# The last six pairs of output tiles of an attention and spectral-mix kernel, dealt out anew among VectorE, ScalarE, GpSimd and the queues

## Chip, cores and metric

One core of one Trainium2 chip. The metric is the device time of one execution in microseconds (us); the kernel before has a median of 435.59 us in three runs (435.58 to 436.14).

## What is computed

Sliding-window causal attention over 8 batches, 8 heads, 576 positions and 64 channels, then a spectral mix of its result. Cut to what matters here:

```python
x = attention(q, k, v)                    # window of 64, as [8, 576, 512]
X = rfft(x, axis=1)[:, :64]               # 64 modes
Y = X @ (w_r + 1j * w_i)                  # one 512 x 512 matrix per mode
y = irfft(Y, n=576, axis=1)
u = x + y
out = u + maximum(u @ w_ch, 0)
```

## The kernel before

The attention, the forward transform and the 64 modes' matmuls fill the first 397 us; they stream the weights from HBM. What this case is about is the rest: the inverse transform and the last line of the reference, which give 36 output tiles of 128 rows by 512 columns in fp32, 256 KB each.

By the time the last modes are done, the product of x with w_ch (`XW[i]`) lies ready in SBUF for every tile. A tile then needs two sums in PSUM. `pu[i]` gets the inverse transform of Y, and `ps[i]` gets XW (`tail_xw`, L812, through an identity matrix) plus the inverse transform of Y @ w_ch. With u = x + pu, the output is u + max(ps, 0).

The tiles go in 18 pairs, in the order of the list `seq`. I call the pairs 0 to 17, and the tiles of pair n "n.0" and "n.1".

- Pairs 0 to 3, 5, 7, 9 and 11 are **early** pairs (`early`, L946): most of their u stands ready in `UE[i]`, in memory that x or the transformed inputs no longer need. VectorE (DVE) adds the last modes' share (`take_u`, L857). Then, but for two tiles that DVE finishes itself (L863), ScalarE (ACT) takes max(ps, 0) out of PSUM into the output buffer (L865) and GpSimd (POOL) adds u to it there (L866).
- Pairs 4, 6, 8 and 10, between them, and 14 to 17, at the end, are **full** pairs. `full_u` (L925) makes u, `full_z` (L935) the output. In pairs 4 to 10 and in the joint pairs, TensorE (PE) adds x through an identity matrix (L876) and ACT copies u out of PSUM (L899). In pairs 14 to 17 this holds for the second tile only; for the first one DVE adds x while it copies (L897). The output, max(ps, 0) + u, is one DVE instruction for each tile (L942).
- Pairs 12 and 13 are the **joint** pairs: each of their four tiles holds the last 64 rows of two batches (tiles 8, 17, 26 and 35, whose x lies in `x4`). Their inverse transform takes two matmuls of 64 rows each (L885).
- Pair 17 is done by `last` (L955). DVE writes 17.0 whole (L968) and 17.1 in two halves.

The order of work is written out by hand, and each engine keeps to the order of its program. The output buffers are seven pairs of tiles, used in turn; the PSUM banks of pu and ps are used anew two pairs later. The outputs leave by DMAs whose issuing engine waits for the tile. SP issues them in the order of a list `plan` that is sorted by a guessed clock: 1.1 us for each early pair and 1.8 us for each other one, and 1.26 us on a second clock for each tile that POOL ends. The second tiles of pairs 12 to 16 (`by_act`) are left out of SP's list; ACT issues them in `send_behind`, one pair later, after its copies of that pair. The second half of 17.1 is ACT's too.

Of the kernel before, what the change touches and what calls it, by code (L numbers as in the profile page):

```python
# [13 lines left out]
ALU = mybir.AluOpType  # L14
ACT_F = mybir.ActivationFunctionType
# [11 lines left out]
def kernel(  # L27
# [10 lines left out]
    nc = tc.nc  # L38
    B, H, S, D = q.shape
    NM = moe_w_r.shape[0]  # L40
    DM = moe_w_ch.shape[0]
# [61 lines left out]
    for at, (grp, hb) in enumerate(steps):  # L103
        for ri in range(2):
            p = 4 * grp
# [89 lines left out]
    with tc.manual_schedule():  # L195
# [184 lines left out]
        for nm in ("k", "q", "v"):  # L380
# [9 lines left out]
                                in1=at.unsqueeze(2).to_broadcast([128, NTC, NM]), op0=ALU.mult, op1=ALU.mult)  # L390
# [7 lines left out]
                         op0=ALU.max, op1=ALU.min)  # L398
# [323 lines left out]
        UE = {}  # L722
# [52 lines left out]
        def tile_of(b, c):  # L775
            return 9 * (b // 2) + 4 * (b % 2) + c
# [25 lines left out]
        for n, pair in enumerate(seq):  # L802
            early = pair[0] in UE_OF
            clock[0] += 1.1 if early else 1.8
            for j, i in enumerate(pair):
                if early and (n, j) not in BY_DVE:
                    clock[1] = max(clock[1], clock[0]) + 1.26
                plan.append((clock[1] if early and (n, j) not in BY_DVE else clock[0], n, i))
        plan = [i for _, _, i in sorted(plan)]
        done = {}  # L810

        def tail_xw(n, js=(0, 1)):  # L812
            for i in [seq[n][j] for j in js]:
                ps[i] = bank("zt"[n % 2 == 0])
                nc.tensor.matmul(out=ps[i], lhsT=ident_r, rhs=XW[i], start=True, stop=True)  # L815

        def banks_u(n):
            for j, i in enumerate(seq[n]):
                pu[i] = bank("m" if n % 2 == 0 else "yp"[j])
# [12 lines left out]
                nc.tensor.matmul(out=ps[i], lhsT=trigLr[r, b % 2, at:at + 128], rhs=ZL[r], start=False, stop=True,  # L832
                                 skip_group_check=True, tile_position=(group_z(b), 0))

        by_act = {p[1] for p in X4 + BB[:-1]}
        behind = []

        def send(i, ut):
            done[i] = ut
            if i in by_act:  # L840
                behind.append(i)
# [9 lines left out]
        def send_behind():  # L851
            while behind:
                put_out(nc.scalar, behind.pop(0), 0, DM)

        def take_u(n):
            for i in seq[n]:
                nc.vector.tensor_tensor(out=UE[i], in0=pu[i], in1=UE[i], op=ALU.add)  # L857

        def take_z(n):
            ut = new_ut()  # L860
            for j, i in enumerate(seq[n]):
                if (n, j) in BY_DVE:
                    nc.vector.scalar_tensor_tensor(out=ut[:, j], in0=ps[i], scalar=0.0, in1=UE[i], op0=ALU.max, op1=ALU.add)  # L863
                else:
                    nc.scalar.activation(out=ut[:, j], in_=ps[i], func=ACT_F.Relu)  # L865
                    nc.gpsimd.tensor_tensor(out=ut[:, j], in0=UE[i], in1=ut[:, j], op=ALU.add)  # L866
            for j, i in enumerate(seq[n]):
                send(i, ut[:, j])

        add_x = {p[0]: "dve" for p in BB}  # L870

        def rows_u(of):
            for i in of:
                if i not in add_x:
                    for h in range(2):
                        nc.tensor.matmul(out=pu[i][:, HALF * h:HALF * h + HALF], lhsT=ident_bf, rhs=tiles[i][0][:, h],  # L876
                                         start=(h == 0), stop=True, skip_group_check=True)
                if len(tiles[i][1]) == 1:
                    (at, b), = tiles[i][1]
                    nc.tensor.matmul(out=pu[i], lhsT=trigI[:, at:at + 128], rhs=yrows(b), start=(i in add_x), stop=True,  # L880
                                     skip_group_check=True)
            for i in of:
                if len(tiles[i][1]) == 2:
                    for h, (at, b) in enumerate(tiles[i][1]):
                        nc.tensor.matmul(out=pu[i][64 * h:64 * h + 64], lhsT=trigI[:, at + 64 * h:at + 64 * h + 64], rhs=yrows(b),  # L885
                                         start=(i in add_x), stop=True, skip_group_check=True, tile_position=(0, 64 * h))
            for i in of:
                b = tiles[i][1][0][1]
                if len(tiles[i][1]) == 2 and b < NLB:
                    r = slice(group_y(b), group_y(b) + 32)  # L890
                    nc.tensor.matmul(out=pu[i], lhsT=trigX[r], rhs=YL[r], start=False, stop=True, skip_group_check=True,
                                     tile_position=(group_y(b), 0))

        def take_rows(i, ut):
            by, halves = add_x.get(i), [t.rearrange("p (h e) -> p h e", h=2) for t in (ut, pu[i])]
            if by == "dve":
                nc.vector.tensor_tensor(out=halves[0], in0=halves[1], in1=tiles[i][0], op=ALU.add)  # L897
            else:
                nc.scalar.copy(out=ut, in_=pu[i])  # L899
# [15 lines left out]
        def new_ut():  # L915
            nonlocal taken_uts
            if not homes:
                homes.append(utpool.tile([128, 2, DM], FP32, name="utx"))
            elif taken_uts == len(homes) < NUT:
                t = ringA.tile([128, 4, DM], FP32, name="ut", tag="wt")  # L920
                homes.extend([t[:, 0:2], t[:, 2:4]])
            taken_uts += 1
            return homes[(taken_uts - 1) % NUT]

        def full_u(n):  # L925
            banks_u(n)
            ut = uts[n] = new_ut()
            for of in [seq[n]] if len(tiles[seq[n][0]][1]) == 2 else [(i,) for i in seq[n]]:
                rows_u(of)
                for i in of:  # L930
                    take_rows(i, ut[:, seq[n].index(i)])
            send_behind()
            tail_xw(n)

        def full_z(n):  # L935
            ut = uts[n]
            for i in seq[n] if len(tiles[seq[n][0]][1]) == 2 else ():
                rows_z(i)
            for j, i in enumerate(seq[n]):
                if len(tiles[i][1]) == 1:  # L940
                    rows_z(i)
                nc.vector.scalar_tensor_tensor(out=ut[:, j], in0=ps[i], scalar=0.0, in1=ut[:, j],  # L942
                                               op0=ALU.max, op1=ALU.add)
                send(i, ut[:, j])

        def early(n, ahead=False):  # L946
# [8 lines left out]
        def last(n):  # L955
            banks_u(n)
            ut = new_ut()
            ut = [ut[:, j] for j in range(2)]
            for j, i in enumerate(seq[n]):
                rows_u((i,))  # L960
                take_rows(i, ut[j])
            send_behind()
            for j, i in enumerate(seq[n]):
                tail_xw(n, (j,))
                rows_z(i)
                for lo in range(0, DM, HALF * (2 - j)):
                    hi = lo + HALF * (2 - j)
                    nc.vector.scalar_tensor_tensor(out=ut[j][:, lo:hi], in0=ps[i][:, lo:hi], scalar=0.0,  # L968
                                                   in1=ut[j][:, lo:hi], op0=ALU.max, op1=ALU.add)
                    done[i] = ut[j]  # L970
                    put_out(nc.scalar if lo else nc.sync, i, lo, hi)
# [85 lines left out]
        for g in (2, 3):  # L1057
            nc.sync.dma_start(out=Zall.bitcast(FP32)[rows, 2 * g:2 * g + 2],
                              in_=ZL.bitcast(FP32)[32 * g:32 * g + 32])
        take_u(0)  # L1060
        take_z(0)
        early(1, ahead=True)
        for n in range(2, len(seq) - 1):
            if seq[n][0] in UE:
# [5 lines left out]
        assert not behind  # L1070
        assert set(plan) == set(seq[-1])

    close(*reversed(opened))
# [30 lines left out]
```

## Time and profile before

| | |
|---|---|
| median of 3 runs | 435.59 us |
| the profiled execution | 437.54 us, its span 435.4 us |
| last matmuls issued by | about 428.2 us |
| last DVE instruction ends | 431.5 us |
| last DMA issue ends (ACT, second half of 17.1) | 432.0 us |
| busy in the whole span | PE 78%, DVE 54%, ACT 41%, POOL 22% |
| POOL's last add ends | 420.9 us |

Every time below is from the start of the span. The profile takes in the first to the last instruction of the program, and the execution has some 2 us around that. DVE's 54% is an average over stages of which this one, the last 8% of the span, has its own bounds. "q" behind an engine's name (SPq, ACTq) is its sequencer: there an issue of a DMA shows, together with its wait.

### The profile page before, as it was taken

How to read it: one execution, taken by the hardware profiler on the slowest of the kernel's cores; microseconds unless marked ns; L12 is line 12 of the kernel's file. 1: busy time of each engine (PE TensorE's matmuls, PEld its weight loads, DVE VectorE, ACT ScalarE, POOL GpSimd, SP SyncE). 2: the span in 40 equal slices, each digit the busy share in tenths (PEclk: the TensorE clock that was granted, in tenths of full speed). 3: DMA queues.
4: the chain of work that ended last, by engine and by line, in shares of the span. 5: the costliest groups of instructions: out<-in, count | busy, mean ns of one | idle time of the engine just before them, and what ended most of it. 6: DMA issues, size and time to landing. Idle time of an engine off the chain costs nothing. (4 is left out here: it accounts for less than half of the span.)

```text
span 435.4 us, 11056 instructions
## 1 busy us (share of the span) xinstructions
PE 337.5 (78%) x4816; PEld 216.8 (50%) x4816; DVE 236.5 (54%) x492; ACT 180.5 (41%) x324; POOL 97.1 (22%) x146
## 2 busy tenths in 40 slices
PE   6989989999999999975217445667557769889993
PEld 3666767676767676652114222344334435445552
DVE  7588777777677676866004111312131326865776
ACT  6556757575666567531202100232121213433651
POOL 8223222222122141113102100021111211111860
PEclk8699999999999999986558655896897989999898
DMA  8999999999999999999999999999999999992796
GB/s 205 211 212 212 211 212 211 212 212 212 211 212 211 212 212 211 212 212 212 211 259 212 212 211 212 212 203 211 213 211 211 213 211 212 212 205 50 288 339 242
DMA packets 46864, 93.24 MB, mean 214 GB/s; under 512 B 2528, under 2 KB 2848, under 8 KB 46816
## 3 DMA queue, kind: packets, MB, share of 16 engines
q0 software_dynamic: 41008, 81.73, 99.2%
q1 hardware_dynamic: 4944, 9.37, 6.0%
q10 hardware_dynamic: 864, 1.44, 0.9%
q8 instruction: 37, 0.61, 0.5%
q14 instruction: 11, 0.09, 0.1%
HBM read 163.58 MB, written 9.44 MB: 397 GB/s over the span
## 5 line engine op out<-in xcount | busy, mean ns | idle before, releaser
L784 DVE CAST xw<-psz 128x512 fp32r<-128x512 f32 x36 | 24.9, 692 | 87.6 <-PE psz L618 87.6
L618 PE MATMUL psz<-wch,tr 128*128 128x512 f32 x176 | 62.2, 485 | 11.6 <-DMA wch<-in_moe_w_ch_dram 11.0
L282 DVE TENSOR_REDUCE mx<-s 128x4 fp32r<-128x512 f32 x72 | 49.5, 688 | 26.8 <-PE s L278 26.6
L586 ACT CAST tr<-ptx 128x512 fp32r<-128x512 bf16 x36 | 21.2, 589 | 98.2 <-PE ptx L611 98.2
L186 PEld LDWEIGHTS <-XQ 128*32 128x32 bf16 x448 | 18.7, 176 | 71.0 <-issue 52.5
L163 POOL DMA_DIRECT2D wi<-in_moe_w_i_dram x32 | 23.4, 732 | 104.0 <-PE psm L186 75.3
L186 PE MATMUL psm<-wi,XQ 128*32 128x512 bf16 x208 | 21.6, 486 | 31.9 <-DMA wi<-in_moe_w_i_dram 31.9
L618 PEld LDWEIGHTS psz<-wch,tr 128*128 128x128 f32 x176 | 36.3, 229 | 19.1 <-issue 11.4
L292 ACT ACTIVATE p<-s 128x512 bf16<-128x512 f32 x72 | 39.7, 603 | 13.9 <-PE s L290 13.9
L163 POOL DMA_DIRECT2D wr<-in_moe_w_r_dram x27 | 20.1, 746 | 91.7 <-PE psm L186 38.1
L186 PE MATMUL psm<-wr,XQ 128*32 128x512 bf16 x184 | 18.9, 485 | 24.2 <-DMA wr<-in_moe_w_r_dram 23.5
L235 ACT COPY kT<-tr 128x576 bf16<-128x576 bf16 x32 | 23.2, 725 | 21.8 <-PE tr L231 21.8
L278 PE MATMUL s<-kT,qT 64*64 64x128 bf16 (+1 forms) x576 | 29.5, 223 | 0.0
L270 PE MATMUL s<-mask_t,ident_bf 128*128 128x512 bf16 x72 | 28.9, 402 | 0.6
L235 ACT COPY qT<-tr 128x576 bf16<-128x576 bf16 x32 | 23.3, 728 | 11.3 <-PE tr L231 11.3
L301 DVE COPY pts<-pt 128x1024 bf16<-128x1024 bf16 (+1 forms) x40 | 25.2, 630 | 4.3 <-PE pt L298 2.6
L278 PEld LDWEIGHTS <-qT 64*64 64x64 bf16 x576 | 18.3, 108 | 18.0 <-issue 17.6
L290 PE MATMUL s<-mx,ident_r 128*128 128x512 f32 x72 | 26.8, 445 | 0.0
L235 ACT COPY vT<-tr 128x576 bf16<-128x576 bf16 x32 | 23.3, 728 | 4.3 <-PE tr L231 4.1
L218 POOL DMA_DIRECT2D rawk<-in_k_dram x15 | 8.1, 539 | 75.2 <-PE tr L231 68.8
L298 PE MATMUL pt<-ident_bf,p 128*128 128x128 bf16 x288 | 23.3, 220 | 1.8 <-issue 1.6
L643 DVE TENSOR_TENSOR stg<-psm,Yfour 128x512 bf16<-128x512 f32 x10 | 6.9, 691 | 31.1 <-PE psm L186 31.0
(242 smaller groups left out, 622.4 us busy)
## 6 DMA issues: line engine op xcount, KB each, us to landing
wi<-in_moe_w_i_dram POOLq DMA_DIRECT2D x29, 1024.0 KB, 17.9
wr<-in_moe_w_r_dram POOLq DMA_DIRECT2D x27, 1024.0 KB, 16.2
out_dram<-ut SPq DMA_DIRECT2D x25, 256.0 KB, 2.2
rawv<-in_v_dram POOLq DMA_DIRECT2D x16, 288.0 KB, 14.7
rawk<-in_k_dram POOLq DMA_DIRECT2D x15, 288.0 KB, 12.5
rawq<-in_q_dram POOLq DMA_DIRECT2D x15, 288.0 KB, 12.4
x_sb<-in_moe_w_r_dram POOLq DMA_DIRECT2D x2, 1024.0 KB, 15.8
out_dram<-utx SPq DMA_DIRECT2D x5, 256.0 KB, 2.5
```

Source lines behind the costliest of these rows:

```text
L163: nc.gpsimd.dma_start(out=w[:, to:to + len(ps)], in_=src[ps[0]:ps[-1] + 1, HALF * hb:HALF * hb + HALF, :].rearrange("g (p j) e -> p g j e" ...
L186: nc.tensor.matmul(out=ps[32 * g:32 * g + 32, 0:e], lhsT=of.rearrange("k s b m -> k (s b) m")[:, (3 * j + 1 - ri) * B:(3 * j + 5 - ri) * B ...
L235: nc.scalar.copy(out=to, in_=pt.rearrange("p j n -> p n j"))
L270: nc.tensor.matmul(out=s, lhsT=ident_bf, rhs=mask_t[:, mk], start=True, stop=True)
L278: nc.tensor.matmul(out=s[ro, t, lo:128], lhsT=lq, rhs=kT[ro, 64 * n - 64 + lo:64 * n + 64], start=False, stop=True, skip_group_check=True)
L282: nc.vector.tensor_reduce(out=mx, in_=s, axis=AX.X, op=ALU.max, negate=True)
L290: nc.tensor.matmul(out=s, lhsT=ident_r, rhs=mx.unsqueeze(2).to_broadcast([128, 4, 128]), start=False, stop=True, skip_group_check=True)
L292: nc.scalar.activation(out=p[:, 4 * c2:4 * c2 + 4, :], in_=s, func=ACT_F.Exp, scale=EX_SCALE)
L298: nc.tensor.transpose(out=pt[:, t, :], in_=st[u]["p"][:, t, :], identity=ident_bf)
L301: nc.vector.tensor_copy(out=ps[:, 0:nt, :], in_=pt[:, 0:nt, :])
L618: nc.tensor.matmul(out=pz, lhsT=tr[:, c, :], rhs=wch[:, c, :], start=(c == 0), stop=(c == NDCH - 1))
L784: nc.vector.tensor_copy(out=XW[i], in_=multiply(tr))
```

## The change

It touches the last six pairs, 12 to 17, and the order in which SP issues.

- Second tiles of pairs 12 to 16 (now `by_pool`) are finished as in the early pairs: ACT takes max(ps, 0) into the output buffer and POOL adds u there (`take_one`). Their u goes into the `UE` place of the early tiles 0.0, 0.1, 1.0, 1.1 and 2.0, which are no longer needed.
- All four joint tiles get x from DVE (`add_x`), so that PE's eight matmuls with the identity (L876) and ACT's four copies (L899) go for them.
- SP issues all whole outputs; ACT keeps only the last half. `send_behind` and `by_act` go.
- In the clock of SP's list each non-early pair counts 1.7 instead of 1.8 us, and the five second tiles go by POOL's clock. From this come SP's new places: 4.0 and 4.1 now stand ahead of 2.1, 12.0 stands ahead of 11.0 and 11.1, and from there the order is 12.0, 11.0, 11.1, 13.0, 12.1, 14.0, 13.1, 15.0, 14.1, 15.1, 16.0, 16.1, 17.0, first half of 17.1.

The core of the diff:

```diff
+        by_pool = [p[1] for p in X4 + BB[:-1]]
...
-            clock[0] += 1.1 if early else 1.8
+            clock[0] += 1.1 if early else 1.7
             for j, i in enumerate(pair):
-                if early and (n, j) not in BY_DVE:
+                pooled = (n, j) not in BY_DVE if early else i in by_pool
+                if pooled:
                     clock[1] = max(clock[1], clock[0]) + 1.26
-                plan.append((clock[1] if early and (n, j) not in BY_DVE else clock[0], n, i))
+                plan.append((clock[1] if pooled else clock[0], n, i))
...
-        by_act = {p[1] for p in X4 + BB[:-1]}
-        behind = []
...
             while plan and plan[0] in done:
-                i = plan.pop(0)
-                if i not in by_act:
-                    put_out(nc.sync, i, 0, DM)
+                put_out(nc.sync, plan.pop(0), 0, DM)
...
+        def take_one(i, ut, u, pooled):
+            if pooled:
+                nc.scalar.activation(out=ut, in_=ps[i], func=ACT_F.Relu)
+                nc.gpsimd.tensor_tensor(out=ut, in0=UE[i], in1=ut, op=ALU.add)
+            else:
+                nc.vector.scalar_tensor_tensor(out=ut, in0=ps[i], scalar=0.0, in1=u, op0=ALU.max, op1=ALU.add)
...
-        add_x = {p[0]: "dve" for p in BB}
+        add_x = {i for p in X4 for i in p} | {p[0] for p in BB}
...
         def take_rows(i, ut):
-            by, halves = add_x.get(i), [t.rearrange("p (h e) -> p h e", h=2) for t in (ut, pu[i])]
-            if by == "dve":
+            if i in by_pool:
+                ut = UE[i] = UE[seq[by_pool.index(i) // 2][by_pool.index(i) % 2]]
+            halves = [t.rearrange("p (h e) -> p h e", h=2) for t in (ut, pu[i])]
+            if i in add_x:
                 nc.vector.tensor_tensor(out=halves[0], in0=halves[1], in1=tiles[i][0], op=ALU.add)
             else:
                 nc.scalar.copy(out=ut, in_=pu[i])
...
-            send_behind()
             tail_xw(n)
...
-                nc.vector.scalar_tensor_tensor(out=ut[:, j], in0=ps[i], scalar=0.0, in1=ut[:, j],
-                                               op0=ALU.max, op1=ALU.add)
+                take_one(i, ut[:, j], ut[:, j], i in by_pool)
```

Line numbers in the text are those of the kernel before.

More of the change, by code (lines that the diff above doesn't have):

```diff
@@ L833, in late_z @@
                                  skip_group_check=True, tile_position=(group_z(b), 0))
-        by_act = {p[1] for p in X4 + BB[:-1]}
-        behind = []
         def send(i, ut):
             done[i] = ut
-            if i in by_act:
-                behind.append(i)
             while plan and plan[0] in done:
-                i = plan.pop(0)
-                if i not in by_act:
-                    put_out(nc.sync, i, 0, DM)
+                put_out(nc.sync, plan.pop(0), 0, DM)
         def put_out(by, i, lo, hi):
@@ L849, in put_out @@
             by.dma_start(out=places[S * b + at:S * b + at + 128, lo:hi], in_=done[i][:, lo:hi])
-        def send_behind():
-            while behind:
-                put_out(nc.scalar, behind.pop(0), 0, DM)
         def take_u(n):
@@ L861, in take_z @@
             for j, i in enumerate(seq[n]):
[L862 to L866, printed above, removed]
+                take_one(i, ut[:, j], UE[i], (n, j) not in BY_DVE)
             for j, i in enumerate(seq[n]):
                 send(i, ut[:, j])
-        add_x = {p[0]: "dve" for p in BB}
+        add_x = {i for p in X4 for i in p} | {p[0] for p in BB}
         def rows_u(of):
@@ L961, in last @@
                 take_rows(i, ut[j])
-            send_behind()
             for j, i in enumerate(seq[n]):
@@ L1063 @@
         for n in range(2, len(seq) - 1):
-            if seq[n][0] in UE:
+            if seq[n][0] in UE_OF:
                 early(n)
@@ L1069 @@
         last(len(seq) - 1)
-        assert not behind
         assert set(plan) == set(seq[-1])
```

## The prediction, as it was made before the changed kernel ran

> **What bounds the end now.** I read the chain of waits first, in order of time. Its columns are start, us, engine, tile and line.
>
> ```profile
> 426.52 0.24 PE pst L908
> 426.76 0.06 issue
> 426.82 0.68 DVE ut L942
> 427.50 0.61 DVE ut L897
> ...
> 431.22 0.33 DVE ut L968
> ```
>
> Up to 426.8 the chain is PE without a gap, from there DVE alone. PE's last matmul starts at 428.2; DVE ends 3 us behind it. The timeline of DVE shows how a pair is spent (start, busy us, line, tile, count, idle before):
>
> ```profile
> 422.19 1.29 DVE L942 SCALAR_TENSOR_TENSOR ut<-psz,ut 128x512 f32<-128x512 f32 x2 [0.90 <-PE psz L905]
> 423.40 0.68 DVE L897 TENSOR_TENSOR utx<-psm,x_sb 128x512 f32<-128x512 f32 x1
> 424.19 1.32 DVE L942 SCALAR_TENSOR_TENSOR utx<-pst,utx 128x512 f32<-128x512 f32 x2
> 425.43 0.68 DVE L897 TENSOR_TENSOR ut<-psy,x_sb 128x512 f32<-128x512 f32 x1
> ...
> 430.19 1.35 DVE L968 SCALAR_TENSOR_TENSOR ut<-psz,ut 128x512 f32<-128x512 f32 x3
> ```
>
> From 422.2 on DVE never rests. Starts give its prices: 0.60 from one instruction to the next (422.19, 422.80, 423.40 in the trace), 0.79 where an instruction reads what the one before it wrote (423.40 to 424.19). A plain pair costs it 0.60 + 0.79 + 0.61 = 2.0, while PE needs 1.6 (pair 14's matmuls start at 422.0, 15's at 423.6, 16's at 425.2).
>
> Next, the windows: length, then busy us (and count) of PE, PEld, DVE, ACT and POOL, granted clock, DMA share, GB/s.
>
> ```profile
> 411.00:420.00 9.00, 9.00 (x54) 5.02 (x53) 7.20 (x12) 6.33 (x13) 8.15 (x8) 1.00 1.01 373
> 420.00:423.00 3.00, 3.00 (x18) 1.54 (x17) 2.10 (x4) 1.07 (x2) 0.91 (x1) 1.00 0.95 351
> 423.00:426.00 3.00, 3.00 (x17) 1.98 (x16) 2.90 (x5) 1.09 (x2) 0.00 (x0) 1.00 0.73 269
> 426.00:429.00 3.00, 2.58 (x13) 1.52 (x11) 2.79 (x6) 1.18 (x2) 0.00 (x0) 1.00 0.89 329
> ```
>
> Two things: POOL is idle from 421 on, and ACT two thirds. And the DMA engines are full (share 1.01, 373 GB/s) until 420; they get air only because DVE then delivers too slowly. In the trace's packets, tiles that queue behind each other start 0.69 us apart (418.27, 418.96, 419.64, 420.33, 421.02).
>
> Last, the output DMAs' own view, and POOL's adds:
>
> ```profile
> DMA to landing us min/median/max: 2.0/2.1/4.5
> 418.40 2.51 POOL L866 TENSOR_TENSOR ut<-XQ,ut 128x512 f32<-128x512 f32 x2 [0.29 <-DVE XQ L857]
> ```
>
> A DMA lands 2.05 us after its issue starts if nothing is ahead of it. The last is ACT's, at 431.62, landing at 433.68; the last 1.75 us to 435.43 are final waits and stay. So the sum asks for the new last landing. A POOL add takes 1.28, one starting 1.23 after the other.
>
> **Part by part.**
>
> *PE.* Eight matmuls (L876) for the joint tiles go. In the chain they take 0.54 for pair 12 and 0.33 + 0.22 for pair 13, together 1.1. PE's start of pair 12 stays at 417.3, since what comes before is untouched. So z is complete for pairs 12 to 16 at 419.4, 421.05, 422.75, 424.35 and 425.95, and for 17.0 and 17.1 at 427.15 and 427.6. The banks it needs are free by then in the schedule below, so PE waits for nobody new.
>
> *DVE.* Five L942 go (second tiles of 12 to 16), four x adds come (joint tiles): one instruction fewer, and the waits for PE and ACT (1.16 and 0.90) close, since the adds fill them. The joint adds have no row of their own; the nearest is L897, same shapes and types, 0.68. From its last L857 (418.17) DVE is back to back: 12.0 and 12.1 add x at 418.77 and 419.37, 12.0 output 419.98; pair 13 the same at 420.6, 421.2, 421.8; then for each plain pair an add and an output, 0.60 + 0.79: outputs of 14.0, 15.0, 16.0 start at 423.2, 424.6, 426.0, 17.0 at 427.4, the halves at 428.0 and 428.3. It ends at 428.7 instead of 431.55: 2.8 earlier. Every z above is there in time, so DVE, not PE, sets this chain.
>
> *ACT and POOL.* Four copies and five issues go from ACT; five of max(ps, 0) come (L865, 0.60). They follow z: ends at 420.05, 421.75, 423.45, 425.05. There is a new wait: 16.1's u goes to a place inside x_sb, and in the built program ACT's copy waits for DVE's x add of 16.0 (ends 425.86), and DVE's x add of 17.0 waits for that copy (ends 426.5). DVE has 16.0's output to do in between, so its cost to DVE is nothing to 0.05; without that cover it would be 0.7. Queued behind ACT's wait is max(ps, 0) of 16.1, which moves to 426.4–427.0. POOL comes free at 420.9 and adds: 12.1 ready 422.1, 13.1 423.35, 14.1 424.85, 15.1 426.45, 16.1 428.4.
>
> *SP.* It takes five issues more, 0.33 each, at least 0.42 apart. It is blocked by a tile not ready: 12.0 (ready 420.66) now stands ahead of 11.0 (419.69), so SP idles from 419.0 to 420.7. 16.1 (428.4) stands ahead of 17.0 (428.05) and the first half of 17.1 (428.4): these issue at 428.42, 428.85 and 429.27. Against ACT's half, issued at 428.7, this costs half a microsecond. The earlier reordering holds 2.1 behind 4.0 and 4.1 (409.24), which leaves one tile more in the DMA queue, 0.69, until pairs 12 and 13 slow the supply. No output buffer is asked for again before some 2 us after that, so it costs nothing by itself.
>
> *DMA engines.* From 12.0 on, 13 whole tiles and two halves have to pass, 14 x 0.69 = 9.66. The first packets of 12.0 go 1.15 after its issue, at 421.85; the queue ahead is empty at about 421.5, so 0.4 is lost there. By the ready times above a gap opens only before 16.1 (0.2). So the transfers end at 421.85 + 9.66 + 0.2 = 431.7, the last landing shows at about 431.85. That is 1.8 before 433.68, not 2.8: the DMA engines, full again, give back 1.0 of DVE's gain.
>
> Sum against the profiled execution: span 435.43 - 1.83 = 433.6, execution 437.54 - 1.83 = 435.7; the median of the runs lies 1.95 below the profiled execution, so 435.59 - 1.83 = 433.8.
>
> On the transfer rate the Trainium skill has another price: DMA: Bandwidth & Descriptors, Specifications, puts the HBM limit of one core at some 358 GB/s. By that a tile takes an estimated 0.73, the 14 tiles 0.6 more, and the median would be 434.4. The windows show 373 GB/s over 9 us, and I stay with them.
>
> **Bounds of the unknown costs.** DVE's joint add: 0.60 (L897) to 0.79 (the dependent step) each; four of them, up to 0.8 late, of which the DMA queue hides part. It gives no gain below 0.60, as no DVE row of this shape is shorter. The PE saving: 0.9 to 1.1, since 0.1 of a switch of weights may pass to L885; DVE's chain hides it. POOL beside DVE and ACT: 1.27 to 1.31 in 14 adds; the last add alone counts. The DMA queue: if supply spreads the load better, the bound is SP's last issue, 429.27, plus 2.0: 431.3, a gain of 2.4. If each tile takes the 0.70 of 373 GB/s and SP loses another gap like that before 12.0 (0.4), the gain is 1.3.
>
> **Rivals.**
>
> *The queue costs nothing* and issue and DVE's chain decide: 433.2, or 432.8 if 16.1 also holds nobody up (17.1's half at 428.7 lands at 430.8, limit by DVE 2.8). For it: landings after 422 are mostly 2.0 to 2.1 behind their issues. Against it: these come from the slack that the change uses up.
>
> *The DMA engines bound it harder.* SP stands still at each tile out of turn, and every idle stretch of full DMA engines is lost. Three more stretches like that before 12.0 cost 1.2: 435.0. For it: one queue now has all whole tiles. Against: the order follows the ready times within 0.5.
>
> *GpSimd becomes the bound; slower.* 16.1 stands ahead of 17.0 and 17.1 on SP, so five adds in line from 420.9 decide the end once they take 2.0 each: 16.1 at 430.9, the last half 0.85 later, landing 2.0 after that, at the 433.7 of before. At twice the row, 2.56, 16.1 comes at 433.7, the last landing at 436.6, 2.9 late: 438.5. The spans of POOL are rough, but SP's issues follow them within 0.02 (419.68, 419.71). Against: 14 adds of the same form at 1.28 beside the same instructions of DVE and ACT. The Trainium skill's GPSIMD Engine Reference, section 4.1, advises against two-input adds here, as about twice as slow as on DVE. The trace agrees (1.28 to 0.68), but the slower engine is the idle one.
>
> *Nothing is gained*, because the throttle takes PE to half speed in the tail, as at 404 to 407.6 (windows of 3.4 us): PE then loses 1.7, and 0.6 of it passes PE's lead of 1.1 over DVE (17.1's z at 427.6, DVE's end at 428.7): at most 434.4. Two windows pass 2.3, DVE ends at 431.0, the last issue comes at some 431.5, as before: 435.5. In this stage the trace shows one window, and none after 408.
>
> **How the numbers follow.** A measurement here can tell about 0.2% (0.87 us) from no change. Forecast, DMA-bound, 433.2 to 434.4: 0.55. The free queue, 432.7 to 433.2: 0.13. Bound harder, 434.4 to 435.4: 0.16, of which 0.08 is still faster than 434.7. Nothing gained: 0.06. GpSimd, slower: 0.10. That is faster 0.55 + 0.13 + 0.08 = 0.76, same 0.08 + 0.06 = 0.14, slower 0.10. The range that leaves out about 2 in 10 is 432.8 to 435.2: above it lie GpSimd, nothing gained and the end of the harder bound.
>
> **What would show it.** In the changed profile: DVE back to back from 418 to about 428.7; PE's last matmul near 427.2; POOL adds of 1.28 ending near 428.4; DMA share near 1 from 422 to 431; SP's last whole issue near 428.9. If the DMA share stays near 0.8 while the end is late, the order of SP is to blame; if DVE shows idle time, the waits I put at nothing; if POOL's adds are longer, the GpSimd rival. A median above 435 would make the working wrong.

## The result, and the profile after

The kernel after has a median of 434.26 us in nine runs (433.58 to 435.45), the kernel before 436.14 us in nine (435.58 to 438.12). The ratio of the means is 0.9949, with a 95% interval of 0.993 to 0.9967. So the change gains 1.9 us by the medians, 1.4 to 3.1 by the interval.

The profiled execution took 434.48 us with a span of 432.45, against 437.54 and 435.43. Not all of this difference of 2.98 in the span is the change's. Before, the throttle holds PE at half speed for 3.4 us from 404.2 on, ahead of the last six pairs; after, it does not do so there. I therefore count from a point that the change leaves alone: the start of pair 11's last two matmuls (L832 before, L834 after), which I call z0. It lies at 416.90 before and 415.77 after (and anywhere from 414.91 to 417.22 in the traces of the experiments), so 1.13 of the 2.98 is spent before the changed part begins. The rest, counted from z0 in us:

| | before | after | difference | predicted |
|---|---|---|---|---|
| PE ends | 11.67 | 10.58 | -1.09 | -1.1 |
| DVE ends | 14.64 | 11.78 | -2.86 | -2.85 |
| POOL's add of 16.1 ends | none | 11.45 | | 11.5 |
| last issue ends | 15.06 | 13.15 | -1.91 | -2.36 |
| last landing | 16.78 | 15.47 | -1.31 | -1.83 |
| 14 of 16 shares landed | 16.74 | 14.95 | -1.79 | |
| final waits behind the last landing | 1.75 | 1.21 | -0.54 | 0 |
| end of the span | 18.53 | 16.68 | -1.85 | -1.83 |

The row "14 of 16 shares" needs a word. Each output leaves 16 landing records in the trace, one for each of the 16 DMA engines, and a tile has landed when the last of them is there. The row has the time by which every output has 14 of its 16. Before, the last records of the last tile come within 0.04 us of one another (the last three). After, the fifteenth is there at 14.98 and the sixteenth only at 15.47. Which engine is late, the records do not say. This late share matters in several experiments.

The end of the chain of waits after (start, us, what):

```profile
424.76 0.02 issue
424.78 0.59 ACT x_sb L895
425.38 0.03 issue
425.41 0.70 DVE ut L893
...
426.20 0.21 DVE ut L961
...
427.22 0.33 DVE ut L961
```

L893 is the old L897 (DVE adds x), L895 the old L899 (ACT's copy), L961 the old L968 (pair 17's outputs). The last instruction starts at 427.22 instead of 431.22. ACT's copy of 16.1's u has come into the chain: DVE's add of x to 17.0 starts 0.03 behind its end. DVE's timeline shows the same stretch (start, busy us, line, tile):

```profile
418.24 0.68 DVE L893 TENSOR_TENSOR x_sb<-psm,x 128x512 f32<-128x512 f32 x1
418.84 0.68 DVE L855 SCALAR_TENSOR_TENSOR ut<-pst,ut 128x512 f32<-128x512 f32 x1
...
421.23 0.68 DVE L893 TENSOR_TENSOR utx<-psm,x_sb 128x512 f32<-128x512 f32 x1
422.01 0.69 DVE L855 SCALAR_TENSOR_TENSOR utx<-pst,utx 128x512 f32<-128x512 f32 x1
422.62 0.68 DVE L893 TENSOR_TENSOR ut<-psy,x_sb 128x512 f32<-128x512 f32 x1
...
425.41 0.69 DVE L893 TENSOR_TENSOR ut<-psy,x_sb 128x512 f32<-128x512 f32 x1
426.20 1.35 DVE L961 SCALAR_TENSOR_TENSOR ut<-psz,ut 128x512 f32<-128x512 f32 x3
```

The line at 418.24 is a joint add: 0.68 long and 0.60 apart from the next, like every other add. There is no idle time in brackets. POOL does what ACT and DVE did before:

```profile
422.32 1.28 POOL L853 TENSOR_TENSOR utx<-XQ,utx 128x512 f32<-128x512 f32 x1
423.86 1.28 POOL L853 TENSOR_TENSOR ut<-XQ,ut 128x512 f32<-128x512 f32 x1 [0.26 <-ACT ut L852]
425.95 1.27 POOL L853 TENSOR_TENSOR ut<-x_sb,ut 128x512 f32<-128x512 f32 x1 [0.81 <-ACT ut L852]
```

Its adds are as long beside a busy DVE as they were before, and before the last one it even waits 0.81 for ACT. The windows (length; busy us and count of PE, PEld, DVE, ACT, POOL; clock; DMA share; GB/s), and the outputs' delay from issue to landing in the whole span after:

```profile
420.00:423.00 3.00, 3.00 (x17) 2.03 (x15) 2.90 (x6) 2.32 (x4) 2.96 (x3) 1.00 0.92 337
423.00:426.00 3.00, 3.00 (x17) 2.12 (x16) 2.79 (x5) 1.81 (x4) 1.93 (x3) 1.00 1.04 382
426.00:429.00 3.00, 0.34 (x2) 0.00 (x0) 1.45 (x4) 0.35 (x1) 1.22 (x1) 1.00 0.99 360
```

```profile
DMA to landing us min/median/max: 2.0/2.6/3.2
```

In the three windows the computing engines run out of work while the DMA engines stay nearly full: a share of 1.04 and 0.99 where before had 0.73 and 0.89. The median delay is 2.6 where all outputs of before have 2.2, so tiles stand in line. Two short stretches are not full, one ahead of 12.0 and one ahead of 16.1:

```profile
420.00:420.50 0.50, 0.50 (x5) 0.41 (x4) 0.50 (x2) 0.50 (x1) 0.50 (x1) 1.00 0.36 131
428.00:428.25 0.25, 0.00 (x0) 0.00 (x0) 0.00 (x0) 0.00 (x0) 0.00 (x0) 1.00 0.62 221
```

### The profile page after: what moved, and what is told of

Read it like the earlier page. It is cut to its first block, busy times and chain, and to the rows that moved or that the text cites. A ratio compares the mean times of both kernels' runs of the same rounds, so it can differ in the third digit from the quotient of the medians.

```text
span 432.5 us, 11043 instructions
## 1 busy us (share of the span) xinstructions
PE 335.0 (77%) x4808; PEld 216.5 (50%) x4808; DVE 236.3 (55%) x491; ACT 181.1 (42%) x325; POOL 103.3 (24%) x151
## 5 line engine op out<-in xcount | busy, mean ns | idle before, releaser
L618 PEld LDWEIGHTS psz<-wch,tr 128*128 128x128 f32 x176 | 37.2, 234 | 19.3 <-issue 11.4
## 6 DMA issues: line engine op xcount, KB each, us to landing
rawv<-in_v_dram POOLq DMA_DIRECT2D x16, 288.0 KB, 15.1
x_sb<-in_moe_w_r_dram POOLq DMA_DIRECT2D x2, 1024.0 KB, 16.1
```

The costliest lines, as they stand in the source:

```text
L618: nc.tensor.matmul(out=pz, lhsT=tr[:, c, :], rhs=wch[:, c, :], start=(c == 0), stop=(c == NDCH - 1))
```

## The experiments

Each run is one profile, read from z0 as above, and timed runs against the kernel before on the same chip.

| run | DVE ends | POOL ends | last issue ends | last landing | final waits | end | 14 shares | 8-KB packet |
|---|---|---|---|---|---|---|---|---|
| before | 14.64 | 4.00 | 15.06 | 16.78 | 1.75 | 18.53 | 16.74 | 18.04 |
| after | 11.78 | 11.45 | 13.15 | 15.47 | 1.21 | 16.68 | 14.95 | 13.20 |
| e1 POOL alone | 12.63 | 12.12 | 13.84 | 16.46 | 1.21 | 17.67 | 15.89 | 14.22 |
| e2 DVE's adds alone | 14.77 | 4.02 | 15.19 | 16.91 | 1.76 | 18.67 | 16.86 | 18.20 |
| e3 SP's issues alone | 14.61 | 4.01 | 15.06 | 16.74 | 1.27 | 18.01 | 16.70 | 14.38 |
| e4 ACT issues 16.1 | 11.79 | 11.46 | 12.41 | 15.33 | 1.34 | 16.67 | 14.82 | 13.10 |
| e5 eight early unsent | 11.78 | 11.45 | 12.80 | 15.06 | 1.28 | 16.34 | 14.96 | 16.80 |
| e6 longer POOL | 11.78 | 13.08 | 14.80 | 17.12 | 1.21 | 18.33 | 16.38 | 14.85 |
| e7 order restored | 11.78 | 11.45 | 13.16 | 15.45 | 1.21 | 16.66 | 14.93 | 13.19 |
| e8 e4 and e7 | 11.78 | 11.45 | 12.36 | 15.15 | 1.33 | 16.48 | 14.64 | 12.92 |
| e9 two issues to ACT | 11.79 | 11.46 | 13.17 | 15.64 | 1.22 | 16.86 | 15.07 | 14.37 |
| e10 e8 and e9 | 11.79 | 11.46 | 12.37 | 15.48 | 1.28 | 16.76 | 14.71 | 14.31 |
| e11 before, two issues more | 14.62 | 4.02 | 15.03 | 17.07 | 1.29 | 18.36 | 16.76 | 16.50 |
| e12 e8, six late unsent | 11.79 | 11.46 | 12.39 | 14.63 | 1.73 | 16.36 | 14.61 | 16.04 |

"14 shares" is the time by which every output has 14 of its 16 landing records. "8-KB packet" has to do with the late share. Behind z0 each trace has two packets of 8 KB in queue 14, which the profile calls "instruction"; the column has the start of the second. Wherever a share falls behind by 0.15 us or more in these tails, it begins with the first or second landing after such a packet starts (in e1 once after one of 16 KB), and it goes on for several tiles where the DMA engines are full. In after the first packet starts at 7.64: the outputs whose 14 shares are there at 7.86 and 8.62 have one that is 0.35 and 0.58 late, and the lag is gone with 16.1, ahead of which the engines are not full. The second packet starts at 13.20, and the last three landings have a share some 0.5 late again. In the ten runs in which the second packet comes ahead of the last shares, the last landing is 0.32 to 0.77 behind the 14 shares, but for e3 (0.04), where the DMA engines have air. In the four others it is at most 0.11 behind. This is a coincidence in time in all the traces; no run moves the packet alone.

### The parts of the change, each alone

**e1: POOL ends the second tiles and SP issues, but PE and ACT still make the joint tiles' u.**

```diff
-        add_x = {i for p in X4 for i in p} | {p[0] for p in BB}
+        add_x = {p[0] for p in BB}
```

> The changed kernel, but the four joint tiles get x from PE and ACT as before; POOL still ends the five second tiles and SP issues all whole outputs. Times are counted from the start of pair 11's last two matmuls (L832 before, L834 after); there before has DVE's end at 14.6, POOL's at 4.0, the last landing at 16.8, and after 11.8, 11.5 and 15.5. Theory (DVE's chain set the end; the fewer outputs it makes are the gain, PE's saving only matters once DVE is shorter than PE): PE ends 1.1 later than in after and now paces DVE: DVE's end 12.9, POOL's 12.4, landing 16.1 to 16.5, so a third to a half of the gain is left. Rival (PE's shorter work is the gain): DVE's end and landing as before, 14.6 and 16.8. Rival (the queues are the gain: ACT no longer holds outputs back): landing as after, 15.5.

Median 435.11 against 436.22, ratio 0.9965 (0.9942 to 0.9989). DVE ends at 12.63, POOL at 12.12, the last landing comes at 16.46. Now PE paces the end (DVE waits for it 1.49 once and 0.31 twice), and ACT, which has the four copies too, feeds POOL:

```profile
423.15 1.29 POOL L853 TENSOR_TENSOR ut<-x_sb,ut 128x512 f32<-128x512 f32 x1 [0.67 <-ACT ut L852]
424.87 1.29 POOL L853 TENSOR_TENSOR utx<-XQ,utx 128x512 f32<-128x512 f32 x1 [0.43 <-ACT utx L852]
426.42 1.29 POOL L853 TENSOR_TENSOR ut<-XQ,ut 128x512 f32<-128x512 f32 x1 [0.25 <-ACT ut L852]
428.06 1.28 POOL L853 TENSOR_TENSOR ut<-x_sb,ut 128x512 f32<-128x512 f32 x1 [0.36 <-ACT ut L852]
```

POOL waits for ACT before each of them. A quarter of the landing's gain is there (0.32 of 1.31); by the 14 shares it is 0.85 of 1.79.

**e2: on the kernel before, only the joint adds go to DVE.**

```diff
-        add_x = {p[0]: "dve" for p in BB}
+        add_x = {p[0]: "dve" for p in BB} | {i: "dve" for p in X4 for i in p}
```

> The kernel before, with one thing of the change: DVE adds x of all four joint tiles, so PE's eight matmuls and ACT's four copies for them go. DVE still makes all outputs, ACT still issues its five. Counted from the start of pair 11's last two matmuls. Theory (DVE's chain): DVE does 4 more instructions of 0.60, but the two waits of 1.2 and 0.9 for PE and ACT close, so DVE's end is 14.8 and the landing 16.9, no gain, though PE ends 1.1 earlier. Rival (PE's shorter work is the gain): DVE's end about 13.5, landing 15.7.

Median 435.95, ratio 0.9982 (0.9959 to 1.0005). PE's eight matmuls are gone, and DVE ends at 14.77 against 14.64. Windows of 14.8 us that begin at z0, first of this run, then of the kernel before:

```profile
414.91:429.71 14.80, 11.32 (x54) 5.46 (x54) 14.36 (x25) 3.44 (x6) 4.03 (x4) 1.00 0.87 320
```

```profile
416.90:431.70 14.80, 11.68 (x63) 6.41 (x62) 12.18 (x21) 5.50 (x10) 3.72 (x3) 0.99 0.84 310
```

PE and ACT have less to do, DVE has four instructions more (25 against 21) in place of its waits, and the outputs come no sooner. Relieving an engine that does not bound the end gave nothing measurable. Both parts together, however, give 1.31 at the landing, where 0.32 and -0.13 would add up to 0.19 (by the 14 shares 1.79, where 0.85 and -0.12 would give 0.73): with POOL's help alone PE becomes the bound, with PE relieved alone DVE stays it.

**e3: on the kernel before, SP issues all whole outputs.**

```diff
-        by_act = {p[1] for p in X4 + BB[:-1]}
+        by_act = set()
```

> The kernel before, with one thing of the change: SP issues all whole outputs in the order of its list, ACT only the last half. Counted from the start of pair 11's last two matmuls. Theory (DVE's chain): nothing changes at the end, DVE's end 14.6, landing 16.8 within 0.1. Rival (the queues are the gain): the landing comes forward by up to 1.3, to 15.5, with DVE's end where it was or earlier.

Median 435.39, ratio 0.9975 (0.9952 to 0.9998). DVE's end and the last landing stay (14.61, 16.74). Yet the span ends 0.52 earlier, since the final waits take 1.27 instead of 1.75. That was not expected, and it is explained below, under the pause of SP.

### What holds the last landing

The prediction said: the DMA engines, full from 12.0 on. The rival was SP, which issues 17.0 only behind 16.1.

**e4: ACT issues 16.1, ahead of its half of 17.1.**

```diff
-        plan = [i for _, _, i in sorted(plan)]
+        plan = [i for _, _, i in sorted(plan) if i != by_pool[-1]]
...
+                    if lo:
+                        put_out(nc.scalar, by_pool[-1], 0, DM)
                     put_out(nc.scalar if lo else nc.sync, i, lo, hi)
```

> The changed kernel, but 16.1, which POOL ends last, is issued by ACT just before its half of 17.1, so that it stands in front of nothing on SP. Counted from the start of pair 11's last two matmuls, after has SP's last issue done at 13.2 and the last landing at 15.5. Theory (behind DVE's chain, SP's order gives part of the gain back: 17.0 and 17.1 wait behind 16.1): 17.0 issues 0.3 us after DVE ends it, the last issue is done near 12.3, the landing near 14.9. Rival (the DMA engines are full, so that the order of issues does not count): landing 15.5 within 0.15.

Median 434.01, ratio 0.9935 (0.991 to 0.996). The last issue ends 0.74 earlier, the last landing only 0.14, the 14 shares 0.13. My theory had asked for 14.9. ACT's half lands 3.35 after its issue starts.

**e5: the outputs of the eight tiles of pairs 4, 6, 8 and 10 are left unsent.**

```diff
-                put_out(nc.sync, plan.pop(0), 0, DM)
+                i = plan.pop(0)
+                if not any(i in seq[n] for n in (4, 6, 8, 10)):
+                    put_out(nc.sync, i, 0, DM)
```

> The changed kernel without the DMAs of the eight tiles of pairs 4, 6, 8 and 10, which are computed but not sent; so the DMA engines have time to spare. Counted from the start of pair 11's last two matmuls, after has DVE's end at 11.8 and the last landing at 15.5. Theory (the DMA engines, full from 408 on, give back part of DVE's gain): DVE's end stays at 11.8, tiles land 2.0 to 2.2 behind their issue instead of 2.6 to 3.0, and the last landing comes at 14.8, bound by SP's last issue. Rival (the transfers are hidden; only the engines and SP's order decide): the last landing stays at 15.5 within 0.15.

Median 433.8 against 436.07, ratio 0.9948 (0.9931 to 0.9965). The landing comes 0.41 earlier, at 15.06, between the two. But the 14 shares land at 14.96, as in after (14.95), so that what this run gains is the late share. The edit takes 16 records from SP besides the transfers, SP's last issue ends 0.35 earlier, and the second 8-KB packet moves behind the last landing. Emptying the queue ahead of 12.0 changes nothing for the other shares: the last tiles fill it anew, and the delay from issue to landing from 420 on has a median of 2.7 here.

**e7: SP's old order for 2.1, and 11.0 and 11.1 ahead of 12.0.**

```diff
+        for i, k in ((seq[2][1], seq[4][0]), (seq[11][1], seq[12][0]), (seq[11][0], seq[11][1])):
+            plan.remove(i)
+            plan.insert(plan.index(k), i)
```

> The changed kernel with SP's list put back in two places: 2.1 ahead of 4.0 and 4.1, and 11.0 and 11.1 ahead of 12.0. Counted from the start of pair 11's last two matmuls. Theory (full DMA engines, every idle stretch of them is lost): the pause of SP before 4.0 and the one before 12.0 go, together 0.5 to 0.7 of idle transfer time, and the last landing comes 0.2 to 0.5 earlier, 15.0 to 15.3, limited by 16.1 on SP. Rival (the order of SP's list in the middle does not count): 15.5 within 0.15.

Median 434.55, ratio 0.9965 (0.9947 to 0.9984); the landing at 15.45, as after. The order of those issues costs nothing that I can see. My theory had expected up to half a microsecond. The time that is saved ahead of 12.0 is lost again ahead of 16.1: the DMA engines' share stays at 0.85 or more from 419.0 to 428.5 and falls to 0.32 for the next 0.5 us.

**e8: e4 and e7 together.**

> The changed kernel with both orders: SP's list put back in the two places, and 16.1 issued by ACT ahead of its half of 17.1. Counted from the start of pair 11's last two matmuls. Theory (full DMA engines, every idle stretch of them is lost, and 16.1 in front of 17.0 is the next limit): last issue done at 12.4, last landing 14.7 to 15.0, 0.5 to 0.8 ahead of after, the fastest of all. Rival (the transfers are a fixed row from 408 on, which no order shortens): landing 15.3, as with 16.1 alone moved.

Median 434.01, ratio 0.9948 (0.9928 to 0.9967). The landing at 15.15 lies between the two numbers. A last issue that ends 0.79 earlier than after's brings 0.32.

**e12: e8 with the outputs of pairs 12, 13 and 14, six tiles, left unsent.** This asks the question directly: are the transfers of the last tiles what the last landing waits for?

```diff
-                put_out(nc.sync, plan.pop(0), 0, DM)
+                i = plan.pop(0)
+                if not any(i in seq[n] for n in (12, 13, 14)):
+                    put_out(nc.sync, i, 0, DM)
```

> Built on the run with both orders and ACT issuing 16.1 (last issue at 12.4 us from the start of pair 11's last two matmuls, last landing 15.15, 2.8 behind). The outputs of the six tiles of pairs 12, 13 and 14 are left unsent; all computing stays. Theory (the transfers from 12.0 on bound the end): with six of fourteen tiles' worth gone the queue is empty when the last tiles come, each landing shows 2.0 to 2.3 behind its issue, and the last landing falls to 14.4 to 14.7, 0.5 to 0.8 earlier, with the last issue still near 12.4. DVE's end stays at 11.8, POOL's at 11.45. Rival (the last landings lag for something other than the queue, such as several engines' issues meeting or the end of the stores' completion): the lag of 2.8 stays and so does 15.1. SP's pause of 0.43 us ahead of its 80th record falls behind the issues, so the final waits may come to 1.3 to 1.75.

Median 433.6 against 435.87, ratio 0.995 (0.9934 to 0.9965). The last issue ends at 12.39 as in e8 (12.36), and the landing comes at 14.63 instead of 15.15. Windows of e8, then of e12:

```profile
423.00:426.00 3.00, 3.00 (x17) 2.09 (x16) 2.79 (x5) 1.85 (x4) 1.94 (x3) 1.00 1.03 378
426.00:429.00 3.00, 0.31 (x2) 0.00 (x0) 1.41 (x4) 0.31 (x1) 1.18 (x1) 1.00 1.01 374
```

```profile
423.00:426.00 3.00, 2.76 (x14) 1.68 (x12) 2.79 (x5) 1.76 (x4) 1.93 (x3) 1.00 0.43 160
426.00:429.00 3.00, 0.00 (x0) 0.00 (x0) 0.97 (x3) 0.00 (x0) 0.65 (x1) 1.00 0.90 324
```

The computing engines do the same, the DMA engines are no longer full from 423 to 426, and with issues that end at the same time the last tile lands half a microsecond earlier. Yet this does not show that the six tiles' transfers held it. The 14 shares land at 14.61 here and at 14.64 in e8, and the half microsecond is that of late shares (two of them in e8). The edit also takes 12 records from SP: the second 8-KB packet moves from 12.92 to 16.04, behind the last landing, and the first one starts at 6.87, when no output is passing. 17.0, which meets an empty queue, lands 2.04 after its issue. The three behind it (16.1 and the halves of 17.1) still show 2.57 to 2.73; they are issued within 0.5 us of each other. So for the tiles of pairs 12 to 14 the answer is no, unless it is their transfers that keep a late share from catching up; this run moves both and can't tell.

What holds the other shares are the last three tiles (16.1, 17.0 and 17.1). An estimate: the first of them lands 2.05 behind its issue, the two behind it 0.69 later each. In after, e5 and e7 the first is 16.1, issued at 11.48 as POOL's last add ends (11.45): 11.48 + 2.05 + 1.38 = 14.91, and the 14 shares are there at 14.93 to 14.96. In e8 and e12 it is 17.0, issued at 11.15: 14.58, against 14.64 and 14.61. In e10 it is 0.12 more than the estimate. In e4, which keeps the gap ahead of 12.0, it is 0.24 more, so there the row from 12.0 on still counts.

### GpSimd's price

**e6: POOL does a half add (into a spare tile) ahead of each of its five adds for the second tiles.**

```diff
+        spent_add = consts.tile([128, DM // 2], BF16, name="spent_add")
...
+            if i in by_pool:
+                nc.gpsimd.tensor_tensor(out=spent_add, in0=UE[i][:, 0:HALF], in1=UE[i][:, 0:HALF], op=ALU.add)
```

> The changed kernel with one GpSimd add more, of half a tile (256 columns, some 0.65 us) into a spare place, before each of the five adds of pairs 12 to 16, so that POOL takes some 1.9 for each of these tiles instead of 1.25. Counted from the start of pair 11's last two matmuls. Theory (POOL has 1.2 us to spare in pairs 12 to 15, and from there 16.1 holds back 17.0 and 17.1 on SP one for one): POOL's end moves from 11.5 to about 13.4, the last landing from 15.5 to about 16.3, still ahead of the 16.8 of before; 2.0 to 2.2 per tile would be the point from which nothing is left. Rival (POOL is not on the path): the landing stays at 15.5. DVE's end stays at 11.8 in both; if DVE's instructions get longer than 0.69 beside a busier POOL, the two engines disturb each other.

Median 435.27, ratio 0.9982 (0.9966 to 0.9998). POOL's timeline:

```profile
424.75 0.62 POOL L854 TENSOR_TENSOR spent_add<-XQ 128x256 bf16<-128x256 f32 x1
425.32 1.29 POOL L857 TENSOR_TENSOR ut<-XQ,ut 128x512 f32<-128x512 f32 x1
426.55 0.63 POOL L854 TENSOR_TENSOR spent_add<-x_sb 128x256 bf16<-128x256 f32 x1
427.12 1.27 POOL L857 TENSOR_TENSOR ut<-x_sb,ut 128x512 f32<-128x512 f32 x1
```

One tile now takes POOL 1.80 (425.32 to 427.12). Its end moves by 1.63, the last landing by 1.65, from 15.47 to 17.12, and the 14 shares by 1.43. The new landing is later than before's 16.78, though the shorter final waits still leave the end of the span 0.20 ahead of before's. My theory had put the landing at 16.3; 0.74 of the 17.12 is the late share. DVE's instructions stay at 0.68 beside POOL's. Five tiles at 0.52 more would be 2.60; 0.97 of that goes into the waits for ACT (0.26 and 0.81 in after). So by this estimate the landing is back at before's value when a tile costs POOL 1.28 + (1.31 + 0.97) / 5 = 1.74; by the 14 shares, with 1.79 for 1.31, it is 1.83.

### The pause of SP

In 13 of the 14 traces SP stands still for 0.43 to 0.46 us ahead of its 80th recorded instruction, and nothing that this instruction waits for comes as late. The exception is e5 (82 records): there the 80th lies behind the last landing and may wait for the other engines' end, and the final waits are 1.28 all the same. In e11 the 80th waits for a landing (1.10 us), and a pause can't be told from the wait. What differs is what this instruction is. Before and in e2 (88 records on SP) it lies behind the last landing, from 433.89 to 434.33 before, and the final waits take 1.75. After (98 records) it lies between two issues, as SP's timeline shows (start and us of each, with its wait):

```profile
427.24 0.33 SPq L844 DMA_DIRECT2D out_dram<-ut  x1
...
428.10 0.33 SPq L844 DMA_DIRECT2D out_dram<-ut  x1
```

These are 16.1 and 17.0, 0.86 apart, though 17.0 has been ready since 426.9. The final waits then take 1.21. In all 14 traces the second 8-KB packet starts 0.5 to 1.8 us after the 80th instruction's start. Whether it belongs to the pause is not shown.

**e9: on the kernel after, ACT issues two early tiles, so that SP has three records fewer.**

```diff
+        first_two = [seq[0][1], seq[1][1]]
...
+            while n == 2 and first_two:
+                put_out(nc.scalar, first_two.pop(0), 0, DM)
```

> The changed kernel, but the outputs 0.1 and 1.1, which DVE ends early, are issued by ACT during pair 2, when ACT has time; SP keeps the rest of its order. So SP has four instructions fewer ahead of 16.1. In all traces so far SP pauses 0.44 us for nothing that the profile shows ahead of its 80th instruction; in after this falls between the issues of 16.1 and 17.0, in before among the final waits behind the last landing. Counted from the start of pair 11's last two matmuls. Theory (the pause hangs on the place in SP's program): it moves behind SP's last issue, where SP waits anyway; 17.0 issues 0.43 behind 16.1 instead of 0.85, the last issue is done at 12.7 instead of 13.15, the last landing at 15.1 to 15.2 instead of 15.47, and the final waits stay at 1.2. Rival (the pause comes of ACT's issue at that moment, or of 16.1): it stays, landing 15.5.

Median 434.57 against 436.42, ratio 0.995 (0.9931 to 0.997). The pause moves behind 17.0, to 428.35 to 428.80, right ahead of the first half of 17.1. So it follows the count. But it still delays the last issue, which ends at 13.17, and the landing at 15.64 is no better (0.57 of it is the late share). The edit moved the count too little to win anything.

**e10: e8 and e9 together (93 records).**

> The changed kernel with all three: SP's list put back in two places, 16.1 issued by ACT ahead of its half of 17.1, and 0.1 and 1.1 issued by ACT during pair 2. Counted from the start of pair 11's last two matmuls. Theory (the DMA engines are full from 12.0 on, so orders and pauses at the end count little once 17.0 and 17.1 are issued in time): the two halves of 17.1 are issued within 0.1 of DVE's end at 11.8, last issue done at 12.3, last landing 14.9 to 15.1, against 15.15 with the two orders alone. Rival (each 0.43 of SP counts in full): 14.7. The final waits stay at 1.2 to 1.3.

Median 433.86 (433.55 to 434.38), ratio 0.9933 (0.9907 to 0.9959). The pause falls at 427.20, into the wait for landings, and costs nothing; the final waits take 1.28. The landing at 15.48 does not follow: the 14 shares are there at 14.71, near e8's 14.64, and the last share comes 0.77 later, behind the second 8-KB packet (14.31). This kernel has the lowest median of those that send all outputs, but its interval overlaps after's, so it is not shown to beat it.

**e11: on the kernel before, two of ACT's issues go to SP (92 records).**

```diff
-        by_act = {p[1] for p in X4 + BB[:-1]}
+        by_act = {p[1] for p in BB[:-1]}
```

> The kernel before, with SP issuing 12.1 and 13.1 as well (ACT keeps 14.1, 15.1 and 16.1), so SP has four instructions more, and its 80th comes ahead of the wait for the last landings instead of behind it. Counted from the start of pair 11's last two matmuls. Theory (the pause hangs on the place in SP's program): DVE's end 14.6 and last landing 16.8 as before, final waits 1.3 instead of 1.75, so 0.4 to 0.5 off the end with no other change. Rival (the final waits are shorter because ACT issues nothing whole any more): final waits 1.75.

Median 435.3, ratio 0.9976 (0.9956 to 0.9995). SP's 80th instruction now lies in the wait for landings, where a pause would cost nothing, and the final waits fall from 1.75 to 1.29. Nothing else of the change is in this kernel. The landing came 0.29 later than before's (17.07), so the profile's end gains only 0.17. By the 14 shares it came 0.02 later; the rest is the late share, with the second 8-KB packet at 16.50. e12 shows the other direction: with 84 records on SP the pause is behind the last landing again, at 430.15, and the final waits are back at 1.73.

## Why the prediction was right, and where not

**The forecast** of 433.8 had 435.59 for before; the nine runs of before have 436.14. The change itself was put at -1.83, and the medians give -1.88. So the 0.46 between 433.8 and 434.26 is nearly all the base.

**This closeness hides two misses that cancel, which is luck.** The last landing moved by -1.31 instead of -1.83, and the final waits, which were to stay, fell by 0.54.

**The landing: the sum has no term for one DMA engine that falls behind.** Its 431.85 is 14.95 from z0. The 14 shares are there at 14.95, the fifteenth at 14.98 and the last at 15.47, so nearly all of the 0.52 is the late share.

That the other shares came out so well is in part luck too. The packets of 12.0 were to start at 421.85 - 416.90 = 4.95, and half of them have started by 4.97 (the first at some 4.6; the starts that the prediction reads are those of the middle of a tile). Ten tiles later (428.47 is 16.1's, 427.62 is 16.0's; 12.0's is 420.74) the pitch is (427.62 - 420.74) / 10 = 0.69, as taken. The last packet ended at 15.0 instead of 14.8, but it is the late engine's; the others' ended at some 14.6. And the last landing shows 0.47 behind the last packet's end (430.77, 431.24), where the sum had 0.15. Before already had 0.35 there (433.33, 433.68), so this was a reading that I could have taken. Packets that end earlier and a longer way from packet to landing cancel. By the Trainium skill's DMA: Bandwidth & Descriptors, Specifications (some 358 GB/s), the median would have been 434.4, nearer to 434.26; but not for its reason, since the window 423 to 426 moves 382 GB/s and the pitch stayed 0.69.

The sum starts its row of transfers at 12.0, and this is not what held the end. By its own gap of 0.2 ahead of 16.1 (some 0.1 in after: a share of 0.62 for 0.25 us) the queue runs empty there, and then nothing ahead of 16.1 counts. e5, e7 and e12 show it: eight tiles fewer, another order ahead of 12.0 and six late tiles fewer leave the 14 shares where they were, to 0.03 (e12 against e8). What counts is 16.1, ready at 11.45 by POOL (11.5 forecast), and the three last tiles.

**"The last 1.75 us are final waits and stay" was wrong.** They contain SP's pause of 0.44. The change adds ten records to SP and thus moves the pause out of them, and the second 8-KB packet with it, from behind the last landing to ahead of the last three. If this packet makes the late share, the landing loses again what the final waits gain. e3 and e11 take 0.48 and 0.46 from the final waits while the landing comes 0.04 earlier and 0.29 later, and e12 gives them back. In after the pause delays the issue of 17.0 by 0.43 (SP's last issue starts at 12.77, forecast 12.37). Little of this reaches the end: e5 has its pause behind the landing and issues 17.0 0.42 earlier, and its 14 shares land 0.01 later.

**DVE's chain held to 0.02**: the joint adds at 0.60, no idle time, the end at 11.78. ACT's copy of 16.1 costs DVE nothing to 0.02, within the 0.05 that was given. PE's saving was 1.09 of 1.1, and e2 shows that it is worth nothing until DVE is relieved; e1, that relieving DVE is worth less than half until PE is. The prediction counted both in one sum without saying that neither works alone.

**SP's reordering costs nothing at the end** (e7). The prediction had said so of 2.1, but had put a loss of 0.4 into its sum for 12.0 ahead of 11.0. That loss came: the DMA engines' share is 0.36 from 420.00 to 420.50, some 0.3 us, and 12.0's packets began 1.00 behind those of the tile ahead instead of 0.69. It does not count, as the gap ahead of 16.1 takes it up.

**The rivals.** "The queue costs nothing" asked for a landing at 431.3, or 14.4 from z0. It fell: the landing was at 15.47 and the 14 shares at 14.95, and e5, whose last issue ends 0.35 earlier, has 14.96. "Bound harder", three more idle stretches, did not occur: there are two gaps, ahead of 12.0 and of 16.1, as forecast. "Nothing is gained" did not occur either; the granted clock is 1.00 until PE's end. GpSimd's adds stayed at 1.28, so that rival fell, but its break-even point of 2.0 was too mild: e6 puts it at 1.74 to 1.83 for the landing. The prediction had the last landing 2.85 behind 16.1's add; e6 shows 4.04 (13.08 to 17.12), with SP's pause of 0.43 and the late share, 0.74, in it. The Trainium skill's GPSIMD Engine Reference, section 4.1, which advises against such adds, agrees with the 1.28 against 0.68, and still the kernel that follows it is the slower one here, as POOL had nothing else to do.

## What to carry to other kernels

When two engines run close behind each other, cost the relief of each alone and of both: here the parts were worth 0.3 and nothing, and together 1.3 (by the 14 shares 0.85, nothing and 1.79). Where the outputs leave at full DMA rate, find the last gap in the transfers: the end is the issue behind it, its way to the landing (2.05 here) and one pitch (0.69) for each tile that follows, and what lies ahead of the gap counts for nothing. Read the 16 landing records of the last tile too, as one late share of 0.5 us decides its landing. Look also at what makes up the time behind the last landing before writing that it stays.

## What was not expected of the hardware

SP stands still for 0.43 to 0.46 us ahead of its 80th recorded instruction in 13 of 14 traces, wherever that instruction lies in time: at 427.2 in e10, at 433.9 before. That it goes with the count is shown, as issues moved to SP or away from it moved the pause (e3, e9, e10, e12). What causes it is not shown by any run. It can be worth 0.4 us at the end of a program, by which side of the last landing it falls on.

One of the 16 shares of a tile lands up to 0.77 us late (in e1 up to 1.93) from the time on at which a packet of 8 or 16 KB of an "instruction" queue starts among the outputs. The traces agree on when; that the packet is the cause is not shown by a run of its own.

The DMA engines of one core moved 382 GB/s from 423 to 426 in after, with one 256-KB tile every 0.69 us.
